# One input load cut by rows, and the output stores cut by batch and by half, in a one-core recurrence and soft-MoE kernel

## Chip, cores and metric

The kernel runs on one core of a Trainium2 chip. The metric is device microseconds (us) of one execution. Beside the times of unprofiled executions there is one profiled execution, from which the views of the trace come; the span is the time from its first to its last instruction.

## The reference

Four sequences of 5056 tokens with 256 channels go through a gated recurrence along the tokens; its output goes through a mixture-of-experts layer with 8 experts of 4 slots each, whose softmaxes run over all 20224 tokens (for the way in) and over the 32 slots (for the way out).

```python
sig = 1.0 / (1.0 + np.exp(-f_logit))
f = lower_bound + (1.0 - lower_bound) * sig
for t in range(S):
    h = f[:, t] * h + (1 - f[:, t]) * x[:, t]
    y[:, t] = h
x = y.reshape(B * S, D)
logits = x @ phi                              # 20224 x 32
d = softmax of logits over the tokens;  c = softmax of logits over the slots
slot_input = d.T @ x                          # 32 x 256
h = relu(slot_input[e] @ w1[e]);  slot_out[e] = h @ w2[e]      # per expert, F = 1024
out = c @ slot_out                            # 20224 x 256
```

All inputs and the output are float32: `x` and `f_logit` 20.7 MB each, the weights 16.8 MB, the output 20.7 MB. No output row can be written before the last weight of the last expert has been used, since every row mixes all slots.

## The kernel before

**First stage, 40 units.** A unit is 512 tokens of one batch. For every pair of units `load` (lines 209 to 226) brings `f_logit` into a tile `f_t` and `x` into a tile `x_t`, on SyncE's DMA queue (SP). Each of the two names has three buffers, so a load waits until the consumer of the tile three pairs earlier is done: ScalarE's sigmoid `gate` (L236, writes `s_t`) for `f_t`, GpSimd's product `enter` (L247, writes `u_t`) for `x_t`. Most pairs are 1024 consecutive tokens of one batch (`long`): one DMA of 128 partitions with 8 KB each, 1 MB (L216). TensorE then turns the tiles to channels on partitions (L251, L266), ScalarE makes the decay `a` (L299, L306), VectorE runs the scan `h` (L334, and L321 for the odd group), TensorE turns `h` back to tokens, and logits, exponentials and slot sums follow. `load(n)` is called six units ahead of its scan. The pair that the change touches, `n = n_unit - 2 * B - 2 = 30`, is the last of the 1 MB pairs; after it come two pairs of 896 KB (L220) and two pairs of two 512 KB DMAs (L226) for each input.

**Weights.** `load_w` (L137, L147) brings the 16 weight tensors (1 MB each in HBM, cast to bfloat16 on the way) on GpSimd's DMA queue. Most of them are issued at the end of the first stage; the last two go into one `f_t` buffer under the name `w_t`, the last of all in two parts of 6/8 and 2/8.

**Experts.** After the slot sums come the two expert products. The last of them, L704, adds up `so_ps` over the experts in order and ends with the two tensors in `w_t`; `slot_out` (L717) is made from it, and `slot_bd` (L719) for two batches side by side.

**Output.** The output of a batch is two blocks of 16 rows per partition (2048 tokens, 2 MB), one block of 7 rows per partition (896 tokens) and 64 tokens left over. TensorE multiplies (L737, L785, L826), VectorE and ScalarE scale into an SBUF tile (`ob` for one batch, `oc` for two), and SP stores it. In order: block 0 of batch 0 in five pieces (`pieces`, L774); the block of 7 rows for batches 0 and 1, then for 2 and 3 (`by_rows`, each stored by `both`, L750, as one DMA of 1792 KB); the 64 left-over tokens (`rest`, L860, two DMAs); block 0 of batches 1, 2, 3 (`whole`, L814, 2 MB each); block 1 of batches 0 and 1 (`couple(1, 0)`, stored by `both`, 4 MB); block 1 of batches 2 and 3 (`couple(1, 1)`, two stores of 2 MB, L843, after all 16 rows are scaled). `couple` walks its 16 rows in eight steps `t` of two rows each.

DMAs of SP are given eight completion semaphores in turn, so each one also waits for the landing of the DMA eight places before it.

Of the kernel before, what the change touches and what calls it, by code (L numbers as in the profile page):

```python
# [18 lines left out]
def kernel(  # L19
# [10 lines left out]
    nc = tc.nc  # L30
    B, S, D = x.shape
# [4 lines left out]
    P = 128  # L36
    DC = D // P
    FC = F // P
    R = 4
    G = P * R  # L40
    n_grp = (S + G - 1) // G
    n_unit = n_grp * B
# [3 lines left out]
    def first(g):  # L46
        return g * G if g < n_grp - 1 else S - G

    def used(g):
        return first(g + 1) - first(g) if g < n_grp - 1 else G  # L50
# [11 lines left out]
    blocks = [(i * P * wide_r, wide_r) for i in range(n_blk)]  # L62
# [105 lines left out]
    with tc.tile_pool(name="sp2", bufs=3) as sp2, \  # L168
# [18 lines left out]
        xs, fs, sts, uts, pss, psus, hs, hps, hts, lgs, ets = ({} for _ in range(11))  # L187
# [4 lines left out]
        def long(n):  # L192
            return B <= n and by_pairs(n)

        def place(n):
            if by_pairs(n):
                t, j = divmod(n, 2 * B)
                return 2 * t + j % 2, j // 2
            return divmod(n, B)
# [4 lines left out]
        def tokens(src, n, k):  # L204
            g, b = place(n)
            v = src[ds(b, k), ds(first(g), G)]
            return v.rearrange("b (p r) d -> p b r d", r=R)

        def load(n, k=2):
            for src, dst, tag in ((f_logit, fs, "f_t"), (x, xs, "x_t")):  # L210
                if n % 2 == 0:
                    dst[n // 2] = ld.tile([P, 2, R, D], F32, name=tag, tag=tag)
                t = dst[n // 2]
                if long(n):
                    g, b = place(n)
                    nc.sync.dma_start(  # L216
                        out=t.rearrange("p u r d -> p (u r) d"),
                        in_=src[b, ds(first(g), 2 * G)].rearrange("(p r) d -> p r d", r=2 * R))
                elif n // B == odd:
                    nc.sync.dma_start(  # L220
                        out=t.rearrange("p u r d -> p (u r d)")[:, ds(0, R7 * D)],
                        in_=src[ds(n % B, 2), ds(first(odd), used(odd))].rearrange(
                            "b (p r) d -> p b (r d)", r=R7))
                else:
                    for m in range(n, n + k):
                        nc.sync.dma_start(out=t[:, ds(m % 2, 1)], in_=tokens(src, m, 1))  # L226
# [256 lines left out]
        for n in range(SINGLE):  # L483
            load(n, 1)
        load(SINGLE)
        lb_constants()
        gate(0, 1)
# [13 lines left out]
        for n in range(n_unit):  # L501
            if n < SINGLE - 2:
# [10 lines left out]
                if n % 2 == 0:  # L513
                    unit(load, n + AHEAD)
# [6 lines left out]
            else:  # L521
# [55 lines left out]
                elif not end and by_pairs(n - 1):  # L577
                    if n % B == 0:
                        g = (n - 1) // (2 * B) * 2
# [50 lines left out]
    with tc.tile_pool(name="ew", bufs=1) as ew, \  # L630
# [34 lines left out]
        for q in range(E // Q):  # L665
# [4 lines left out]
            if q == 0:  # L670
                nc.tensor.matmul(cs_ps, rep2, cs1, start=True, stop=True)
                src = ht_ps.rearrange("p f (j s) -> p f j s", s=NS)[:, :, :, ds(0, SPE)]
                src = bass.AP(tensor=src.tensor, offset=src.offset,
                              ap=[list(src.ap[0]), [P, FC], [NS + SPE, Q], [1, SPE]])
                dst = hid[:, :, :, ds(0, SPE)]
                dst = bass.AP(tensor=dst.tensor, offset=dst.offset,
                              ap=[list(dst.ap[0]), [Q * NS, FC], [NS + SPE, Q], [1, SPE]])
# [3 lines left out]
            for j in range(Q):  # L681
                s0 = (Q + j) * SPE
                src = ht_ps[:, :, ds(j * NS + s0, SPE)]
# [40 lines left out]
    with tc.tile_pool(name="osb", bufs=3) as osb:  # L724
# [18 lines left out]
        def rows_of(i, b):  # L743
            t0, n_r = blocks[i]
            return out[ds(b * S + t0, P * n_r)].rearrange("(p r) d -> p r d", r=n_r)

        def both(i, j, ob):
            t0, n_r = blocks[i]
            dst = out.rearrange("(b t) d -> b t d", b=B)[ds(2 * j, 2), ds(t0, P * n_r)]
            nc.sync.dma_start(out=dst.rearrange("u (p r) d -> p u (r d)", r=n_r),  # L750
                              in_=ob.rearrange("p u r d -> p u (r d)"))

        def first_op():
            n = n_ops[0]
# [22 lines left out]
        def by_rows(i, j):  # L777
            t0, n_r = blocks[i]
            k = ds(j * 2 * NS, 2 * NS)
            ew = etall[k, ds(t0, P * n_r)].rearrange("s (p r) -> s p r", r=n_r)  # L780
            scale = rrow[:, ds(t0 // P, n_r), ds(2 * j, 2)]
            ob = osb.tile([P, 2, n_r, D], F32, name="oc", tag="oc")
            for r in range(n_r):
                op = first_op()
                nc.tensor.matmul(op.rearrange("p u d -> p (u d)"), ew[:, :, r],  # L785
                                 slot_bd[k].rearrange("s u d -> s (u d)"),
                                 start=True, stop=True, skip_group_check=True)
                if r % 2 == 0:
                    by_vector(ob[:, :, r], op, scale[:, r].unsqueeze(2))
                else:  # L790
                    for u in range(2):
                        nc.scalar.activation(ob[:, u, r], op[:, u], ACT.Copy,
                                             scale=scale[:, r, ds(u, 1)])
            both(i, j, ob)
# [21 lines left out]
        def couple(i, j):  # L816
            t0, n_r = blocks[i]
            ew = etall[ds(j * 2 * NS, 2 * NS), ds(t0, P * n_r)].rearrange(
                "s (p r) -> s p r", r=n_r)
            scale = rrow[:, ds(t0 // P, n_r), ds(2 * j, 2)]  # L820
            ob = osb.tile([P, 2, n_r, D], F32, name="oc", tag="oc")
            for t, r in enumerate(range(0, n_r, 2)):
                k = min(2, n_r - r)
                op = pout.tile([P, 2, 2, D], F32, name="op", tag="op")
                for i_r in range(k):
                    nc.tensor.matmul(op[:, i_r].rearrange("p u d -> p (u d)"),  # L826
                                     ew[:, :, r + i_r],
                                     slot_bd[ds(j * 2 * NS, 2 * NS)].rearrange("s u d -> s (u d)"),
                                     start=True, stop=True, skip_group_check=True)
                if t % 2 == 0:  # L830
                    nc.vector.tensor_tensor(  # L831
                        ob[:, :, ds(r, k)].rearrange("p u r d -> p r u d"), op[:, ds(0, k)],
                        scale[:, ds(r, k)].unsqueeze(3).broadcast_to([P, k, 2, D]), ALU.mult)
                else:
                    for i_r in range(k):
                        for u in range(2):
                            nc.scalar.activation(ob[:, u, r + i_r], op[:, i_r, u], ACT.Copy,  # L837
                                                 scale=scale[:, r + i_r, ds(u, 1)])
            if j == 0:
                both(i, j, ob)  # L840
                return
            for u in range(2):
                nc.sync.dma_start(out=rows_of(i, 2 * j + u), in_=ob[:, u])  # L843

        def rest():
            n_p = B // 2
# [18 lines left out]
        for i in range(1, end):  # L865
            for j in range(B // 2):
                couple(i, j)
# [30 lines left out]
```

## Time and profile before

| | before |
|---|---|
| median of 3 runs | 196.5 us (196.48 to 199.11) |
| the profiled execution's own time | 196.45 us |
| its span | 194.7 us |
| mean granted TensorE clock | 0.855 |
| HBM read, written | 58.23 MB, 20.71 MB |
| busy share of the span | PE 77%, VectorE 73%, ScalarE 71%, GpSimd 53% |
| last input load of SP issued | 100.0 us |
| last weight load issued | 124.5 us |
| first output store issued | 143.4 us |
| last output store issued | 176.2 us |

Times inside the execution are microseconds from the start of the span. An engine's busy share is a mean over stages that have different limits, so it doesn't say what bounds a stage. The page's second part cuts the span into 40 equal slices of 4.87 us; its line "DMA" gives the mean busy share of the core's 16 DMA engines in tenths (9 is 90% or more), and "GB/s" what they moved, counted where the data is written, so that a weight load that is cast from float32 to bfloat16 counts with half of what it reads.

### The profile page before, as it was taken

To read this page: it belongs to the slowest core of one execution; us is meant where nothing else is said; L and a number is where in the kernel's file an instruction comes from. 1 tells how busy PE (TensorE), PEld (TensorE's weight loads), DVE (VectorE), ACT (ScalarE), POOL (GpSimd) and SP (SyncE) were. 2 spreads that over 40 slices of the span, in tenths; PEclk is the share of its full clock that TensorE was granted. 3 is DMA by queue.
4 is the path that set the end of the run, shared out by engine and by line. 5 is a ranking of instruction groups with operands and counts; after the bars stand their busy time and mean duration, and the time that the engine had idled before them with its cause. 6 is when DMAs were issued, how large, how long until landed. Compare 5 with 4: busy or idle time off the path is not lost.

```text
span 194.7 us, 3266 instructions
## 1 busy us (share of the span) xinstructions
PE 150.1 (77%) x1216; PEld 106.6 (55%) x1216; DVE 142.2 (73%) x175; ACT 138.9 (71%) x193; POOL 102.5 (53%) x77
## 2 busy tenths in 40 slices
PE   0685897998998979899798976999697999980000
PEld 0464666685776767667585865677461764420000
DVE  2666799899899999999999999543178867770000
ACT  3586888799999999899988698531068688991000
POOL 2586788774999688874979979570030000000000
PEclk9999799699999999999999999999995555555555
DMA  5999999999999999999999999999839999999995
GB/s 206 418 429 429 429 426 419 426 431 373 364 424 424 406 333 428 424 422 358 379 416 414 255 217 213 213 214 216 169 148 428 427 450 431 431 431 431 431 431 222
DMA packets 11953, 70.75 MB, mean 363 GB/s; under 512 B 1297, under 2 KB 1682, under 8 KB 7458
## 3 DMA queue, kind: packets, MB, share of 16 engines
q1 hardware_dynamic: 9456, 62.13, 76.4%
q0 software_dynamic: 2480, 8.42, 21.6%
q8 instruction: 9, 0.15, 0.3%
q14 instruction: 6, 0.05, 0.1%
q10 hardware_dynamic: 2, 0.00, 0.0%
HBM read 58.23 MB, written 20.71 MB: 405 GB/s over the span
## 4 chain that ended last, share of the span: by engine, by line
DMA 31%; PE 26%; DVE 22%; ACT 5%; POOL 3%; issue 3%; SPq 1%; ACTq 0%; POOLq 0%
DVE h L334 11%; DMA f_t<-in_f_logit_dram 10%; DMA w_t<-in_moe_w_dram 10%; PE op L826 7%; DMA x_t<-in_x_dram 6%; PE op L737 6%; DMA w_sb<-in_moe_w_dram 5%; POOL u_t L247 3%; PE sp L251 3%; PE hp L347 3%; DVE h L321 3%; DVE ht L366 3%; PE up L266 3%; DVE oc L727 2%; ACT s_t L236 2%
## 5 line engine op out<-in xcount | busy, mean ns | idle before, releaser
L247 POOL TENSOR_TENSOR u_t<-s_t,x_t 128x1024 bf16<-128x1024 bf16 (+1 forms) x39 | 82.3, 2128 | 22.5 <-ACT s_t L236 13.0
L334 DVE TENSOR_TENSOR_SCAN h<-a,h,up 128x512 bf16<-128x512 f32 x64 | 78.1, 1267 | 6.4 <-PE up L266 2.2
L236 ACT ACTIVATE s_t<-f_t 128x2048 bf16<-128x2048 f32 (+2 forms) x23 | 38.2, 1669 | 4.9 <-DMA f_t<-in_f_logit_dram 4.7
L347 PE MATMUL hp<-ident_f,h 128*128 128x128 f32 (+1 forms) x160 | 29.3, 308 | 8.5 <-DVE ht L366 6.5
L347 PEld LDWEIGHTS hp<-ident_f,h 128*128 128x128 f32 (+1 forms) x160 | 23.6, 207 | 17.7 <-DVE ht L366 11.3
L299 ACT ACTIVATE a<-sp,lbs 128x1024 f32<-128x1024 bf16 x28 | 29.7, 1113 | 2.4 <-PE sp L251 2.4
L251 PE MATMUL sp<-ident_f,s_t 128*128 128x128 f32 x144 | 22.1, 298 | 7.1 <-ACT s_t L236 5.8
L266 PE MATMUL up<-ident_f,u_t 64*128 64x64 f32 x224 | 21.1, 233 | 1.9 <-POOL u_t L247 1.9
L251 PEld LDWEIGHTS sp<-ident_f,s_t 128*128 128x128 f32 x144 | 17.7, 152 | 8.8 <-ACT s_t L236 6.5
L731 ACT ACTIVATE ob<-op,rrow 128x256 f32<-128x256 f32 x32 | 12.4, 478 | 11.7 <-PE op L737 11.3
L266 PEld LDWEIGHTS up<-ident_f,u_t 64*128 64x128 f32 x224 | 16.7, 141 | 6.7 <-issue 2.7
L366 ACT COPY ht<-hp 128x512 f32<-128x512 f32 (+1 forms) x21 | 12.2, 581 | 5.6 <-PE hp L347 5.6
L306 ACT ACTIVATE a<-sp,lbs 128x512 f32<-128x512 bf16 (+2 forms) x16 | 13.2, 868 | 3.1 <-PE sp L251 2.8
L185 PE MATMUL slot_ps<-rep,ident_f 128*128 128x256 f32 x42 | 14.3, 431 | 0.0
L366 DVE COPY ht<-hp 128x512 f32<-128x512 f32 (+1 forms) x19 | 12.7, 670 | 1.2 <-PE hp L347 1.1
L826 PE MATMUL op<-slot_bd,etall 64*128 64x512 bf16 x32 | 13.1, 626 | 0.0
L837 ACT ACTIVATE oc<-op,rrow 128x256 f32<-128x256 f32 x32 | 12.2, 486 | 0.8 <-PE op L826 0.3
L737 PE MATMUL op<-slot_out,etall 32*128 32x256 bf16 x64 | 12.6, 374 | 0.1
L831 DVE TENSOR_TENSOR oc<-op,rrow 128x1024 f32<-128x1024 f32 x8 | 9.7, 1223 | 3.4 <-PE op L826 3.4
L727 DVE TENSOR_TENSOR ob<-op,rrow 128x1024 f32<-128x1024 f32 (+2 forms) x12 | 9.9, 862 | 2.2 <-PE op L737 1.1
L737 PEld LDWEIGHTS <-etall 32*128 32x128 bf16 x64 | 9.0, 152 | 4.0 <-issue 1.7
L380 PE MATMUL lg<-h,phi 128*32 128x512 bf16 (+1 forms) x80 | 10.7, 412 | 0.2 <-ACT et L404 0.2
(109 smaller groups left out, 168.3 us busy)
## 6 DMA issues: line engine op xcount, KB each, us to landing
f_t<-in_f_logit_dram SPq DMA_DIRECT2D x14, 1024.0 KB, 12.3
x_t<-in_x_dram SPq DMA_DIRECT2D x14, 1024.0 KB, 10.6
w_sb<-in_moe_w_dram POOLq DMA_DIRECT2D x14, 512.0 KB, 10.3
out_dram<-ob SPq DMA_DIRECT2D x3, 2048.0 KB, 9.7
f_t<-in_f_logit_dram SPq DMA_DIRECT2D x8, 512.0 KB, 8.6
x_t<-in_x_dram SPq DMA_DIRECT2D x8, 512.0 KB, 7.7
out_dram<-oc SPq DMA_DIRECT2D x1, 4096.0 KB, 14.0
out_dram<-oc SPq DMA_DIRECT2D x2, 2048.0 KB, 15.3
```

The lines of the kernel that those rows point to most:

```text
L185: nc.tensor.matmul(slot_bank[:, 1], ident_f, wide_rep, start=first, stop=False, skip_group_check=True)
L236: nc.scalar.activation(s_t, f_t, ACT.Sigmoid, scale=-1.0)
L247: nc.gpsimd.tensor_tensor(uts[n][:, :r], s_t[:, :r], x_t[:, :r], ALU.mult)
L251: nc.tensor.transpose(ps[:, :, r], t[:, r].bitcast(F32), ident_f)
L266: nc.tensor.transpose(v[:, :, r], t(r)[k].bitcast(F32), ident_f[k, k])
L299: nc.scalar.activation(a, sp[:, :, :, :, o], ACT.Identity, scale=nomlb[:, ds(o, 1)], bias=1.0)
L334: nc.vector.tensor_tensor_scan(h[:, :T, o], decays[n // 2, o][:, n % 2, :T], up[:, :T, o], hs[number(g - 1, b)][:, ds(used(g - 1) - 1, 1), ...
L347: nc.tensor.transpose(hp[:n_p, r], hw[:, :n_p, r], ident_f)
L366: copy(hts[g][:n_p, b].rearrange("p r d -> p (r d)").bitcast(F32), hps.pop(n)[:n_p].rearrange("p r c -> p (r c)"))
L727: nc.vector.tensor_tensor(ob, op, scale.broadcast_to(list(ob.shape)), ALU.mult)
L737: nc.tensor.matmul(op[:, j], ew[:, :, r + j], slot_out[ds(b * NS, NS)], start=True, stop=True, skip_group_check=True)
L826: nc.tensor.matmul(op[:, i_r].rearrange("p u d -> p (u d)"), ew[:, :, r + i_r], slot_bd[ds(j * 2 * NS, 2 * NS)].rearrange("s u d -> s (u d)"),
```

## The change

One load is cut by rows, and five stores are cut in two. The load of `f_logit` for the pair `n = 30` becomes four DMAs into the same tile, of partitions 0 to 111, 112 to 117, 118 to 123 and 124 to 127. `both` issues one DMA for each of its two batches. In `couple(1, 1)` the stores go out after the fourth and after the eighth step, each for eight of the 16 rows of one batch: four DMAs of 1 MB in the place of two of 2 MB. No computation on any engine is changed.

```diff
+        LEAN = (112, 6, 6, 4)
+
         def load(n, k=2):
...
                 if long(n):
                     g, b = place(n)
-                    nc.sync.dma_start(
-                        out=t.rearrange("p u r d -> p (u r) d"),
-                        in_=src[b, ds(first(g), 2 * G)].rearrange("(p r) d -> p r d", r=2 * R))
+                    to = t.rearrange("p u r d -> p (u r) d")
+                    at = src[b, ds(first(g), 2 * G)].rearrange("(p r) d -> p r d", r=2 * R)
+                    p = 0
+                    for k_p in LEAN if n == n_unit - 2 * B - 2 and dst is fs else (P,):
+                        nc.sync.dma_start(out=to[ds(p, k_p)], in_=at[ds(p, k_p)])
+                        p += k_p
...
         def both(i, j, ob):
-            t0, n_r = blocks[i]
-            dst = out.rearrange("(b t) d -> b t d", b=B)[ds(2 * j, 2), ds(t0, P * n_r)]
-            nc.sync.dma_start(out=dst.rearrange("u (p r) d -> p u (r d)", r=n_r),
-                              in_=ob.rearrange("p u r d -> p u (r d)"))
+            for u in range(2):
+                nc.sync.dma_start(out=rows_of(i, 2 * j + u), in_=ob[:, u])
...
+                if j and t % 4 == 3:
+                    h = ds(r - 6, 8)
+                    for u in range(2):
+                        nc.sync.dma_start(out=rows_of(i, 2 * j + u)[:, h], in_=ob[:, u, h])
             if j == 0:
                 both(i, j, ob)
-                return
-            for u in range(2):
-                nc.sync.dma_start(out=rows_of(i, 2 * j + u), in_=ob[:, u])
```

SP issues 71 DMAs in the place of 63: 51 loads (48) and 20 stores (15).

## The prediction

> **What bounds the kernel now.** I read the page's slices first: which resource has no room.
>
> ```profile
> DMA  5999999999999999999999999999839999999995
> GB/s 206 418 429 429 429 426 419 426 431 373 364 424 424 406 333 428 424 422 358 379 416 414 255 217 213 213 214 216 169 148 428 427 450 431 431 431 431 431 431 222
> ```
>
> The 16 DMA engines are busy from the second slice on, except in slices 29 and 30 (136 to 146 us). The dips in GB/s are weight loads, of which only the written half is counted. So there are two DMA-bound stretches, all the loads and all the stores, with a short one between. Which work joins them is in the chain that ended last:
>
> ```profile
> 111.58 10.09 DMA w_sb<-in_moe_w_dram
> 121.96 18.77 DMA w_t<-in_moe_w_dram
> 140.77 1.10 PE so_ps L704 x8
> 141.90 0.49 DVE slot_out L717
> 142.44 0.39 PE op L737 x2
> ```
>
> The last weights land at 140.7 us, 18.8 us after their issue: they wait in the queues, not for an issuer. 2.7 us later (143.41) the first store goes out. The loads' drain, in the DMA view cut to 139 to 142 us (40 slices of 75 ns):
>
> ```profile
> DMA  9989979969879642756666453210000000000800
> ```
>
> The engines run dry one by one over more than a microsecond. The trace's 16 increments of the last transfer's semaphore say the same: 139.71 to 141.44 us, three of them within 0.2 us of the first, four at +0.55 to +0.73, one at +1.07, eight at +1.35 to +1.73, mean +1.0. Of the last store's 16 increments (192.97 to 193.77), 15 lie within 0.28 us. Loads end unevenly, stores nearly level.
>
> Why unevenly: until 5 us the increments of one load lie within 0.25 us of each other. Then one engine falls 0.35 us behind, and after 29.7 us one is 1.3 us behind.
>
> ```profile
> q8 instruction: 9, 0.15, 0.3%
> q14 instruction: 6, 0.05, 0.1%
> q10 hardware_dynamic: 2, 0.00, 0.0%
> ```
>
> Nine instruction blocks of 16 KB go through the same engines, each 0.9 to 1.0 us long, at 29.7, 48.0, 62.5, 79.0, 92.5, 104.9, 124.3, 135.2 and 141.8 us; after each of the first eight one more engine is late, and none catches up, as none is ever idle. The last line is the load of the one-partition `lb_row`: one data packet and one completion packet. One partition used one engine.
>
> **Part 1, the load of 112, 6, 6 and 4 rows.** A 128-row load gives each engine 8 packets of 8 KB; 1 MB landings lie 2.455 us apart, so a row is 2.455/8 = 0.307 us. If 112 rows go 7 to an engine and 6, 6 and 4 rows one to an engine, always on the same first engines, then four engines carry 10 rows (+0.61 us), two carry 9 (+0.31) and ten carry 7 (-0.31). No queue is idle from here to 139 us, so the shift stays until the last weights.
> The small parts' own cost: 512 KB loads land 1.240 us apart and 1 MB loads 2.455, so cutting one in two costs 2 x 1.240 - 2.455 = 0.025 us of engine time; three more on the six engines, 0.075 us.
> The end of the loads is that of the latest engines. Bounds: if all the late ones are among the ten, -0.31 us (the others end at most at +0.73 + 0.61 + 0.08 = +1.42, level with 1.73 - 0.31); if one of the latest is among the four, +0.61 + 0.08 = +0.69 us. The trace doesn't number engines. But each packet starts 3 to 4 ns after the one before it on its engine ended, so up to 47 us its packets can be linked to 16 chains. Eight chains begin at 1.75 to 1.81 us, the others from 2.41 us on. Of the first eight, seven are not late at 47 us, and the eighth got an 8 KB instruction block at 44.7 us; the 16 KB block of 29.7 us and the early 0.35 us fell on chains of the second eight. If engines start in their order, the six that get more are among the early seven. I take -0.31.
>
> [...]
>
> **SP's queue at part 1.** Three more issues of 0.33 to 0.38 us stand ahead of the next `x_t` load and of all that follow:
>
> ```profile
> 73.09 0.33 SPq L216 DMA_DIRECT2D x_t<-in_x_dram  x1
> 73.51 0.38 SPq L216 DMA_DIRECT2D f_t<-in_f_logit_dram  x1
> 77.93 0.33 SPq L216 DMA_DIRECT2D x_t<-in_x_dram  x1
> 78.35 0.66 SPq L220 DMA_DIRECT2D f_t<-in_f_logit_dram  x1
> ```
>
> SP waits from 73.89 to 77.93 for GpSimd's `u_t`: 4.04 us of cover for 1.1. Without it the loads would still lie some 10 us deep in the queues (issue to landing 10 to 12 us). The fourth part must also await the landing eight DMAs back, the `x_t` load of 61.15 + 12.3 = 73.5 us: done by then. With three more DMAs the first odd load comes to wait for the `x_t` load issued at 66.44, landed at about 78.5 against its issue at 78.35; behind it in SP's queue is only the next `x_t`, at 82.84. Its tile is read at 93.1 us. Nothing.
> The reader of the cut load, `s_t`, waits for four landings:
>
> ```profile
> 88.00 1.28 ACT L236 ACT_TABLE_LOAD   x1
> 89.30 1.91 ACT L236 ACTIVATE s_t<-f_t 128x2048 bf16<-128x2048 f32 x1
> ```
>
> The load lands at 85.8 and ScalarE, busy without a gap, starts at 89.3: 3.5 us of slack.
>
> **Part 2, the stores.** The order of rows stays; there are five more DMAs. From 144 us the engines always have work: the last stores are issued at 175.8 us, while the 4 MB store before them (issued 170.1, 14.0 us to landing) lands at 184.1. The half that now goes out some 3 us sooner joins a queue 8 us long: gain 0. Cost: 5 x 0.025 = 0.125 us of engine time, taken from loads since no store shows it alone. SP's extra issues (0.38 us, up to 1.21 in a pair) lie ahead of that backlog; SP waits 4.5 us for `oc` there.
> Smaller packets: the halves have 8 KB per partition for 16 KB.
>
> ```profile
> 16.00:29.00 13.00, 9.95 (x67) 7.49 (x66) 10.93 (x11) 10.67 (x11) 9.33 (x7) 0.87 1.01 429
> 146.00:149.00 3.00, 3.00 (x10) 0.79 (x7) 3.00 (x7) 3.00 (x10) 0.00 (x0) 0.50 1.05 434
> 159.00:173.00 14.00, 14.00 (x41) 6.20 (x40) 10.68 (x9) 12.91 (x35) 0.00 (x0) 0.50 1.00 430
> ```
>
> The last column is GB/s: 8 KB loads 429; the pieces of L774, 4 to 6 KB per partition at a pitch of 16 KB, 434; 16 KB stores 430. The nearest row, the pieces, has the halves' pattern: 0. The other end is 4.19 MB at 429 for 430, +0.02 us. One engine ends each late store 0.5 us after the others; halves could take that away at best: -0.5.
>
> [...]
>
> **Sum.** -0.31 + 0.125 = -0.19 us on the profiled execution, 196.45 (span 194.7, 1.75 around it): 196.26. Its median is 0.05 higher, so I say 196.3.
>
> **Rivals.**
> 1. *The lean falls on late engines, or the 112 rows don't run freely* (0.35). Late engines among the six: +0.31 (one of the two) to +0.69 (one of the four), and +0.125: 196.9 to 197.3. For: eight of 16 are late at the end, and six blocks drawn at random would hardly miss them all. Against: the chains up to 47 us. The same comes out if engines slow each other in the 112 rows, so that seven take as long as eight did: nobody gains, and the six carry +0.31 to +0.69 more. [...]
> 2. *A small part goes through one engine* (0.05). Then 16 rows go to one engine, 23 for 8: 15 x 0.307 = +4.6 us. For: `lb_row` did so with one row. Against: 128-row loads spread evenly. The loads end 4.6 us later if that engine was among the latest, 4.6 - 1.73 = 2.9 if the foremost: 199.5 to 201.2. It is slower by over 2% (200.4) when the engine was already over 0.9 us late, as nine of 16 are.
> 3. *Nothing happens* (0.05): later blocks set which engines end last whatever the load did: 196.45 to 196.6.
>
> The forecast has 0.55, with a range of its own from 195.8 (the 0.5 us of the last engine gained) to 196.6. Over 2%, about what a measurement of this kernel can tell from no change, no case is faster: even perfectly level engines would end the loads only 0.7 us sooner. I leave 0.01 for it, 0.04 for slower (most of rival 2), 0.95 for neither. The range holds the forecast and rivals 1 and 3: 195.8 to 197.4.
>
> **What would show it.** Right: the last `w_t` lands about 0.3 us sooner than 140.7, the busy engines of that drain end closer together, the first store goes out near 143.1, the stores keep 430 GB/s. Wrong: the drain is longer and later (rival 1), by 3 us or more (rival 2); a gap in the DMA slices after 146 us, or `s_t` waiting for `f_t` at 89 us, would break my reading of the covers.

## The result, and the profile after

| | before | after |
|---|---|---|
| median of 6 runs | 196.63 us (196.48 to 199.11) | 201.48 us (200.33 to 202.23) |
| ratio, 95% interval | | 1.0235 (1.0201 to 1.027) |
| the profiled execution's own time, its span | 196.45, 194.7 us | 200.56, 198.8 us |
| weights of the chain that ended last landed | 140.73 us | 144.71 us (+3.98) |
| first output store issued | 143.41 us | 147.33 us (+3.92) |
| last store landed | 193.77 us | 197.86 us (+4.09) |
| first store's issue to last store's landing | 50.36 us | 50.53 us (+0.17) |

The changed kernel is slower by 2.35%. The lower half of the table places the loss: the loads end 4.0 us later, and the stores take 0.17 us more than before. The forecast had -0.31 us for the loads and +0.125 us for the stores.

The page's slices and its packet counts, of the kernel after:

```profile
DMA  6999999999999999999999999999929999999995
GB/s 208 413 433 424 424 435 420 429 424 353 384 430 422 380 362 422 336 238 352 382 419 416 275 241 211 214 214 216 186 79 426 428 441 422 425 422 448 420 422 242
DMA packets 12305, 70.75 MB, mean 356 GB/s; under 512 B 1393, under 2 KB 1778, under 8 KB 7554
```

"DMA" says, as before, that the engines are busy: 9 in all slices but the first, the drain's and the last. "GB/s" says that they moved less while busy: slices 17 to 19 (79.5 to 94.4 us) have 336, 238 and 352, where the slices of before show only one weight load's dip. A packet that takes longer counts as busy all the while (a share of 1.03 at 246 GB/s below), so the busy share alone would have hidden the loss.

The same place in stretches of 2 us, and two stretches of stores; the last column is GB/s, the one before it the DMA share:

```profile
82.00:84.00 2.00, 2.00 (x22) 1.76 (x23) 2.00 (x2) 2.00 (x3) 1.09 (x1) 1.00 1.03 246
84.00:86.00 2.00, 2.00 (x18) 1.18 (x18) 2.00 (x3) 1.98 (x3) 0.63 (x1) 1.00 1.02 238
86.00:88.00 2.00, 1.82 (x15) 1.35 (x14) 2.00 (x3) 1.99 (x3) 2.00 (x2) 1.00 1.03 213
88.00:90.00 2.00, 1.99 (x24) 1.60 (x21) 2.00 (x3) 0.24 (x2) 1.98 (x2) 1.00 0.93 314
149.90:152.90 3.00, 2.72 (x9) 0.77 (x8) 3.00 (x7) 3.00 (x10) 0.00 (x0) 0.73 1.05 433
163.00:177.00 14.00, 14.00 (x42) 6.16 (x41) 10.69 (x9) 12.91 (x35) 0.00 (x0) 0.50 1.00 430
```

The four stretches from 82 to 90 us before:

```profile
82.00:84.00 2.00, 2.00 (x22) 1.73 (x22) 2.00 (x3) 2.00 (x3) 0.91 (x2) 1.00 1.03 434
84.00:86.00 2.00, 2.00 (x19) 1.22 (x16) 2.00 (x2) 1.98 (x3) 2.00 (x1) 1.00 1.00 422
86.00:88.00 2.00, 1.82 (x14) 1.35 (x13) 2.00 (x3) 1.98 (x3) 1.98 (x3) 1.00 1.02 431
88.00:90.00 2.00, 1.89 (x24) 1.50 (x21) 2.00 (x4) 1.99 (x2) 0.76 (x1) 1.00 1.01 400
```

The difference, 188 + 184 + 218 + 86 = 676 GB/s over 2 us each, is 1.35 MB, or 3.2 us at 425 GB/s: most of the 3.98. The stores keep their 430 GB/s. The packets say the same one by one: from 81.5 to 90 us 212 of those of 8 KB take 0.547 us (median) and not 0.309; before, none there takes over 0.35. The cut load has only 128, so whole loads beside it are slowed as well. That is 212 x 0.24 / 16 = 3.2 us, the mean of the 16 engines.

Nothing later gives it back. The chain that ended last:

```profile
125.59 19.12 DMA w_t<-in_moe_w_dram
144.75 1.05 PE so_ps L709 x8
145.82 0.49 DVE slot_out L722
146.36 0.39 PE op L742 x2
```

It is the chain of before, with every step about 4 us later. The loads' drain, in the DMA view cut to 142.7 to 145.7 us:

```profile
DMA  7987979698997666223111111110000000000000
```

The tail at the level of one or two engines is longer: the 16 increments of the `w_t` in that chain lie 2.49 us apart, 1.66 before.

### The profile page after: what moved, and what is told of

It is laid out like the page before. It is cut to its first block, busy times and chain, and to the rows that moved or that the text cites. A ratio compares the mean times of both kernels' runs of the same rounds, so it can differ in the third digit from the quotient of the medians.

```text
span 198.8 us, 3280 instructions
## 1 busy us (share of the span) xinstructions
PE 150.1 (76%) x1216; PEld 106.5 (54%) x1216; DVE 142.1 (72%) x175; ACT 138.6 (70%) x193; POOL 102.5 (52%) x77
## 2 busy tenths in 40 slices
DMA packets 12305, 70.75 MB, mean 356 GB/s; under 512 B 1393, under 2 KB 1778, under 8 KB 7554
## 4 chain that ended last, share of the span: by engine, by line
DMA 32%; PE 22%; DVE 12%; ACT 10%; POOL 7%; issue 5%; SPq 2%; ACTq 0%; POOLq 0%
DMA f_t<-in_f_logit_dram 11%; DMA w_t<-in_moe_w_dram 10%; DVE h L339 7%; PE op L829 7%; POOL u_t L252 6%; DMA x_t<-in_x_dram 6%; DMA w_sb<-in_moe_w_dram 6%; PE op L742 6%; ACT s_t L241 4%; PE sp L256 3%; ACT a L304 3%; PE hp L352 3%; DVE oc L732 2%; DVE ht L371 2%; PE up L271 1%
```

## The experiments

The theories that the expectations name by letters: **A**, engines slow each other on the way into SBUF, by which partitions a load covers (the expectations say that they share ports, the author's assumption: the runs show rates and times of packets, and no port; A1 and A2 are two ways of pricing that, told where they are used). **B**: a row costs what the prediction says, and the loss is in the unequal number of rows on the engines. **C**: reading pieces of 7 rows from HBM is slow. **D**, the number of DMAs: each more costs far more than 0.025 us. The edits are shown against the kernel after, or against the one before with its load cut.

### The two halves of the change alone: `stores_only`, `lean_only`

The first is the kernel after with its loads uncut, the second is the kernel before with only the cut load.

```diff
-                    for k_p in LEAN if n == n_unit - 2 * B - 2 and dst is fs else (P,):
+                    for k_p in (P,):
```

> Only the stores are changed, all loads as before. Every theory that puts the loss into the load (A: engines share write ports of SBUF in a load of 112 rows; B: the extra rows went to engines that were already late; C: reading HBM in pieces of 7 rows is slow; D: more DMAs and issues) expects the time of before plus five more DMAs at 0.025 us: 196.6 us, between 196.4 and 196.9. If the stores carry part of the loss, 198 us or more.

> Only the load of 112, 6, 6 and 4 rows is changed, all stores as before. A, B, C and D all expect the time of the changed kernel less 0.1 us, 200.2 to 202.1 us, with packets of that load and of the next one at 0.5 us in the place of 0.309. If load and stores only cost together, 196.5 us.

Measured: `stores_only` 196.96 us against 196.6 (ratio 1.0015, 1.0001 to 1.003), just above the range expected; from first store to last landing 50.54 us in its trace. `lean_only` 200.26 us (1.0184, 1.0167 to 1.02). The load is 3.66 us of the loss, the stores 0.36. In the trace the stores are only 0.18; the stretch between the last landing and the end of the span varies by 0.4 us from one trace here to the next, so the other 0.18 can't be placed.

### Equal rows, and halves: `r112_16`, `r64_64`

The kernel before, with the one load cut otherwise. `ports` below has 2304 packets under 512 B for 144 DMAs of 128, 112, 64 and 16 rows, 16 for each. Read as one for each engine that took part, and with rows dealt evenly, every engine has 7 + 1 = 8 rows of 112 and 16, and 4 + 4 of 64 and 64.

```diff
-        LEAN = (112, 6, 6, 4)
+        LEAN = (112, 16)
```

> The load as two DMAs of 112 and 16 rows: by the packets of the changed kernel each of the 16 engines then carries 7 + 1 = 8 rows, so that no engine gets more than another. A (shared ports) expects the same loss, +2.8 to +4.5 us, 199.3 to 201.1 us. B (uneven lean) expects no loss, 196.5 us. C (pieces of 7 rows) expects +3 us or more, as A. D (more DMAs) expects 1/3 of the loss at most, 197.8 us.

```diff
-        LEAN = (112, 6, 6, 4)
+        LEAN = (64, 64)
```

> The load as two DMAs of 64 rows, 4 rows to an engine in each, 8 in all. A (shared ports): if pairs of engines write one port, 0.614 us a row for those that meet, a loss of +1.8 to +2.7 us, 198.3 to 199.2 us. [...] B expects no loss, 196.5 us. C (pieces of 7 rows, not a power of two) expects none either, 196.5 us, since an engine reads 4 rows in a run. D expects 197.8 us at most.

Measured: 200.3 us (1.0189, 1.017 to 1.0208) and 201.67 us (1.0267, 1.024 to 1.0293). Equal rows lose as much as the uneven ones: B falls as the cause of the loss here. Halves lose 5.1 us, where C expected nothing: C falls. It is the direction of A, but 1.9 to 2.8 times its price (1.8 to 2.7 us). The stretches from 82 to 86 us in `r64_64` (last column GB/s):

```profile
82.00:84.00 2.00, 2.00 (x22) 1.63 (x23) 2.00 (x3) 2.00 (x3) 1.10 (x1) 1.00 1.03 168
84.00:86.00 2.00, 2.00 (x21) 1.25 (x15) 2.00 (x2) 1.98 (x3) 0.00 (x0) 1.00 1.02 209
```

0.39 and 0.50 of the 434 and 422 of before, at a DMA share of 1.03 and 1.02.

### Four DMAs of all 128 rows: `cols4`

The same load as four DMAs, each of 512 of a partition's 2048 elements.

```diff
+        COLS = (512, 512, 512, 512)
...
-                    for k_p in LEAN if n == n_unit - 2 * B - 2 and dst is fs else (P,):
-                        nc.sync.dma_start(out=to[ds(p, k_p)], in_=at[ds(p, k_p)])
+                    for k_p in COLS if n == n_unit - 2 * B - 2 and dst is fs else (2 * R * D,):
+                        nc.sync.dma_start(out=to.rearrange("p r d -> p (r d)")[:, ds(p, k_p)],
+                                          in_=at.rearrange("p r d -> p (r d)")[:, ds(p, k_p)])
```

> The same load as four DMAs again, but cut along its columns: 128 rows of 2 KB each, so that rows and engines stay as in the load of before. A (shared ports), B and C expect no loss beyond 3 x 0.025 us, 196.5 to 196.8 us. D (more DMAs and issues, completions) expects the loss of the changed kernel, 200 us or more.

Measured: 196.93 us against 196.58 (1.0016, 1.0006 to 1.0026), a little above the range expected. The same stretches as above:

```profile
82.00:84.00 2.00, 1.29 (x11) 1.29 (x12) 2.00 (x4) 1.57 (x2) 1.82 (x1) 1.00 1.04 405
84.00:86.00 2.00, 2.00 (x21) 1.06 (x19) 2.00 (x2) 1.66 (x3) 1.05 (x1) 1.00 1.08 448
```

As many DMAs as in the changed load, a tenth of its loss: D falls. What costs is which partitions a DMA covers.

### Each shape by itself: `ports`

The whole computation is left out. Each stage is 16 loads of one shape into 16 places, then a VectorE copy that waits for them; at the end eight stores of a shape. All have 8 KB per partition, on SP's queue.

```python
def stage(parts):
    for n in range(N):
        for a, k in parts:
            nc.sync.dma_start(out=big[ds(a, k), n], in_=src[n, ds(a, k)])
    settle()
```

> A kernel that leaves the whole computation out and measures loads and stores alone: 16 loads each, 8 KB per row, with a drain after each stage: 128 rows; rows 0 to 63; rows 32 to 95; rows 0 to 111; rows 0 to 111 and then 112 to 127; 128 rows again; then 8 stores each of 128 rows, of rows 0 to 63, of rows 32 to 95, of rows 0 to 111. All theories: 425 to 430 GB/s for 128 rows. A (shared ports): 213 GB/s for rows 0 to 63, 420 for rows 32 to 95, which have as many rows and bytes, and about 250 GB/s for 112 rows with or without the 16. [...] C (pieces of 7 rows from HBM): 425 for rows 0 to 63 and for rows 32 to 95, 250 for 112 rows. A third, fewer rows make each load slower by its fixed cost: the same lower figure for rows 0 to 63 and 32 to 95. For the stores A in its strict form (reading SBUF shares ports as well) expects the same three figures; if only writes into SBUF share, 420 to 430 for all four.

Stretches inside the stages, in the order: loads of rows 0 to 127; 0 to 63; 32 to 95; 0 to 111; 0 to 111 and 112 to 127; 0 to 127 again; stores of rows 0 to 127; 0 to 63; 32 to 95; 0 to 111. The last columns are PEclk, DMA share and GB/s:

```profile
4.00:41.00 37.00, 0.00 (x0) 0.00 (x0) 1.00 1.01 423
46.00:85.00 39.00, 0.00 (x0) 0.00 (x0) 1.00 1.02 207
96.00:109.00 13.00, 0.00 (x0) 0.00 (x0) 1.00 1.01 425
114.00:165.00 51.00, 0.00 (x0) 0.00 (x0) 1.00 1.01 271
172.00:234.00 62.00, 0.00 (x0) 0.00 (x0) 1.00 1.02 251
240.00:277.00 37.00, 0.00 (x0) 0.00 (x0) 1.00 1.00 419
282.00:299.00 17.00, 0.00 (x0) 0.00 (x0) 1.00 1.01 426
302.00:320.00 18.00, 0.00 (x0) 0.00 (x0) 1.00 1.00 208
325.00:334.00 9.00, 0.00 (x0) 0.00 (x0) 1.00 0.99 410
340.00:353.00 13.00, 0.00 (x0) 0.00 (x0) 1.00 1.00 362
```

Rows 0 to 63 run at half the rate and rows 32 to 95 at the full one, with the same bytes and as many packets (16 under 512 B for each DMA), loads and stores alike. The stretch of the 425 leaves out the stage's start, which is slower (307, 258 and 270 GB/s from 88 to 94 us); whole stages of loads take 43.38 and 24.13 us. So it is the place of the rows that decides, as A says. A's 213 and 250 were near what the kernel's stretches had shown (168 to 209 GB/s in `r64_64`, 229 to 250 in `r112_16`, from 82 to 88 us); its 420 for rows 32 to 95 was an assumption that no run had shown before this one. Measured are 207, 425, and 271 and 251. The rows read in HBM move along with the partitions here; that the HBM side is the cause is unlikely, since in `r64_64`, with other HBM addresses, a packet takes as long (0.62 us; 0.64 for rows 0 to 63 here), but no run moved one without the other. The 112 rows have 271 GB/s, and with 16 rows after them 251: 112 rows take longer than 128 (0.92 MB at 271 are 3.39 us, 1.05 MB at 423 are 2.48). On the way out 112 rows lose less, 362 of 426, for which A has no price.

### Cut loads among whole ones: `mix`

The computation is left out. In a stage of 16 loads every second one is cut: by none; 112, 16; 112, 6, 6, 4; 64, 64; 32, 64, 32; none.

```python
def mix(parts):
    for n in range(N):
        for a, k in parts if n % 2 else [(0, 128)]:
            nc.sync.dma_start(out=big[ds(a, k), n], in_=src[n, ds(a, k)])
    settle()
```

> A kernel that leaves the whole computation out: six stages of 16 loads of 1 MB each, with a drain after each stage; in a stage every second load is cut by rows and the others are of 128 rows: no cut; 112 and 16; 112, 6, 6 and 4; 64 and 64; 32, 64 and 32; no cut. Alone, 112 and 16 rows ran at 253 GB/s and 64 rows at 204, which is 4.14 and 5.14 us for 1 MB in the place of 2.47. A1 (only the cut load itself pays): +1.7 us for each 112 and 16, +2.7 for each 64 and 64, so stages 13 and 21 us longer than the uncut 40. A2 (the uncut load beside it pays too, since the engines reach it at different times): +3.5 to +5 us for each, stages 28 to 40 us longer. 32, 64 and 32, of which the middle runs at 420 alone: A1 +1.3, A2 +2.5 or more.

VectorE's timeline; the number in brackets is how long it waited for the stage's loads:

```profile
43.23 0.17 DVE L35 COPY mark<-big 128x16 f32<-128x16 f32 x1 [42.34 <-DMA big<-in_f_logit_dram]
100.99 0.17 DVE L35 COPY mark<-big 128x16 f32<-128x16 f32 x1 [57.59 <-DMA big<-in_f_logit_dram]
176.07 0.17 DVE L35 COPY mark<-big 128x16 f32<-128x16 f32 x1 [74.90 <-DMA big<-in_f_logit_dram]
241.40 0.18 DVE L35 COPY mark<-big 128x16 f32<-128x16 f32 x1 [65.16 <-DMA big<-in_f_logit_dram]
308.93 0.17 DVE L35 COPY mark<-big 128x16 f32<-128x16 f32 x1 [67.35 <-DMA big<-in_f_logit_dram]
```

Divided by eight cut loads: +1.9 us for 112, 16; +4.1 for 112, 6, 6, 4; +2.9 for 64, 64; +3.1 for 32, 64, 32. At the rates of `ports`, 1.05 MB cost 1.05/0.251 - 2.48 = +1.7 for 112, 16 and 1.05/0.207 - 2.48 = +2.6 for 64, 64: near what is measured, so that A1 (only the cut load pays) holds for these two and A2 (the load beside it pays too, 3.5 to 5 us) does not. The last shape costs far more than its parts' own rates would (+1.3, if its 32-row parts run at 207 and the middle at 425), so how neighbouring DMAs overlap counts too. And the price of 112, 16 is only half of the kernel's 3.7. For 112, 6, 6, 4, the change's own cut, it is the other way: 4.1 here and 3.66 in the kernel. So unequal rows, which cost nothing extra in the kernel, do cost here (4.1 against 1.9), where a stage has them eight times; whether they fall on the same engines each time, no run shows.

### Where in the kernel, and how often: `r112_early`, `r112_fx`

The first cuts the load of pair 10 in 112 and 16 rows and not that of pair 30; the second cuts both loads of pair 30, `f_t` and `x_t`.

```diff
-                    for k_p in LEAN if n == n_unit - 2 * B - 2 and dst is fs else (P,):
+                    for k_p in LEAN if n == 2 * B + 2 and dst is fs else (P,):
```

> The cut of 112 and 16 rows moved from the last long load (n = 30) to an early one (n = 10), which lands near 25 us, before the first instruction block delays an engine. A1 (a cut load pays by itself): +1.7 us, 198.3 us. A2 with the engines' lags as the cause of the part beyond it: +1.7 to +2.2 us, since the engines lie within 0.6 us of each other there, against 1.7 us at n = 30. A2 without the lags: +3.7 us, 200.3 us, as at n = 30.

```diff
-                    for k_p in LEAN if n == n_unit - 2 * B - 2 and dst is fs else (P,):
+                    for k_p in LEAN if n == n_unit - 2 * B - 2 else (P,):
```

> Both loads of the pair n = 30, f_logit and x, cut into 112 and 16 rows, one right behind the other. If each cut load costs what the one did: 2 x 3.7 = +7.4 us, 204 us. If part of the loss is at the seams to the uncut loads, which are as many as for one cut load: 1.7 + 3.7 = +5.4 us, 202 us.

Measured: 199.01 us (1.0112, 1.0081 to 1.0143), +2.2; and 204.41 us (1.0374, 1.0329 to 1.0419) against 196.78, +7.6, twice `r112_16`'s 3.7. The idea that the cost sits at the seams between a cut and a whole load, which had 202 us for both loads, falls: each cut load pays in full. And the same cut is 1.5 us cheaper early. One thing that differs between the places is how far the engines have drifted apart: before, the 16 increments of the loads ahead of pair 10 lie 0.6 us apart, and around pair 30 1.7.

### The kernel after once more: `after_again`

> The changed kernel once more, on the chip of the other runs of this group. The sum of its parts as measured alone, 3.66 for the load and 0.36 for the stores, is 200.6 us; its median before was 201.5 (200.3 to 202.2). If the parts add up: 200.4 to 201.2; if load and stores cost something together, 201.5 again.

Measured: 200.68 us (1.0206, 1.017 to 1.0241). The two halves of the change add up to it: 196.6 + 3.66 + 0.36 = 200.6. The first result's median was 0.8 higher, with runs spread over 1.9 us; why is open.

### Level engines: `drain_whole`, `drain_cut`

A small store ahead of the load of pair 30 reads the `x_t` tile that is still to land, so that the queue should run dry and all engines start level (the intent; how level they were is not shown). In `drain_whole` the load is whole, in `drain_cut` cut in 112 and 16 rows.

```diff
+                    if n == n_unit - 2 * B - 2 and dst is fs:
+                        nc.sync.dma_start(out=out[ds(0, 1)],
+                                          in_=xs[n // 2 - 1][ds(0, 1), 0, 0].bitcast(F32))
```

> The kernel of before with one small store of 1 KB ahead of the load at n = 30, which waits until the x_t load before it has landed (its row of the output is written again at the end). All engines are then idle when the load at n = 30 goes out, so that none is late for it; the load is whole. Every theory: some 3 us more than before, 199 to 200.5 us, for the empty queue. It is the base of the next run.

> The same with the load at n = 30 cut into 112 and 16 rows. If the engines' lags at the seam in front of the cut load make its cost 3.7 us in the kernel and 2 us in the stages alone: 1.7 to 2.3 us over the run before it (drain_whole). If something else of the kernel does (the loads behind it, the other tensor, the other engines): 3.2 us or more over it.

Measured: 201.98 us (1.0258, 1.0216 to 1.03) and 202.31 us (1.0329, 1.0256 to 1.0401). Running dry costs 5.4 us by itself, where 3 were expected, so only the two are compared. Their medians are 0.3 us apart, the ratios 1.4, with intervals that overlap, and of the two profiled executions the one with the cut is the faster (202.23 for 203.62 us): the whole times don't price the cut. The traces do at its place: by the median of the 16 increments, the cut load lands 1.37 us later after its issue than the whole one, and the `x_t` load behind it 1.41. The same reading of `r112_16` against the kernel before gives 2.1 and 3.1. So the cut costs about 1.4 us behind the drain, less than either range expected, and 2.1 to 3.1 us without it.

### Late engines by themselves: `lags`

The computation is left out. Each stage is ten loads with the third whole, cut (112, 16) or in halves, twice each; ahead of it no other load, then one of 8 rows, then one of 4, which was meant to make 8 or 4 engines late.

```python
def stage(late, third):
    if late:
        nc.sync.dma_start(out=big[ds(0, late), LAG], in_=src[LAG, ds(0, late)])
    for n in range(10):
        for a, k in third if n == 2 else full:
            nc.sync.dma_start(out=big[ds(a, k), n], in_=src[n, ds(a, k)])
    settle()
```

> A kernel that leaves the whole computation out: 18 stages of ten 1 MB loads, each with a drain after it, of which the third is whole, cut into 112 and 16 rows, or cut into 64 and 64; each kind twice; and this without a small load ahead, then with one of 8 rows, then with one of 4 rows ahead of the ten, which makes 8 or 4 of the 16 engines about 1.2 us late. If the part of the loss that the cut load alone doesn't explain comes from engines that reach the seams at different times, the cut costs 1.5 to 1.9 us (112 and 16) and 2.2 to 2.9 us (64 and 64) in the stages without a late engine, and at least 2.5 us (112 and 16) with late engines. If lateness doesn't matter, the cost is the same in all three, within 0.3 us, and the rest of the loss in the kernel has another cause.

VectorE's timeline, whole and cut, first with no load ahead, then with 8 rows ahead:

```profile
28.36 0.18 DVE L36 COPY mark<-big 128x16 f32<-128x16 f32 x1 [27.47 <-DMA big<-in_f_logit_dram]
56.17 0.17 DVE L36 COPY mark<-big 128x16 f32<-128x16 f32 x1 [27.64 <-DMA big<-in_f_logit_dram]
86.20 0.18 DVE L36 COPY mark<-big 128x16 f32<-128x16 f32 x1 [29.85 <-DMA big<-in_f_logit_dram]
115.81 0.17 DVE L36 COPY mark<-big 128x16 f32<-128x16 f32 x1 [29.43 <-DMA big<-in_f_logit_dram]
...
204.98 0.18 DVE L36 COPY mark<-big 128x16 f32<-128x16 f32 x1 [28.44 <-DMA big<-in_f_logit_dram]
233.07 0.18 DVE L36 COPY mark<-big 128x16 f32<-128x16 f32 x1 [27.92 <-DMA big<-in_f_logit_dram]
262.69 0.18 DVE L36 COPY mark<-big 128x16 f32<-128x16 f32 x1 [29.44 <-DMA big<-in_f_logit_dram]
292.96 0.17 DVE L36 COPY mark<-big 128x16 f32<-128x16 f32 x1 [30.10 <-DMA big<-in_f_logit_dram]
```

The cut costs 29.64 - 27.56 = 2.1 us with no load ahead, 29.77 - 28.18 = 1.6 with 8 rows and 1.8 with 4 rows ahead; the halves 2.5, 2.1 and 2.5. But the small load didn't make engines late by the 1.2 us expected, a figure that no run had shown: in the whole stages the 16 increments of the load just ahead of the third lie 0.3 to 0.5 us apart with it and 0.4 to 0.7 without, and ahead of the cut load in `r112_16` 1.8. So the stages give the price of a cut for engines that are nearly level, 1.6 to 2.1 us, and say nothing of late ones.

## Why the prediction was wrong

**What bounds the kernel: right.** Two DMA-bound stretches joined by the last weights; the 3.98 us that the loads lost came out at the end (+4.09).

**The term that failed:** "If 112 rows go 7 to an engine and 6, 6 and 4 rows one to an engine" and its price of 0.307 us a row. The counts agree with the rows: packets under 512 B grew from 1297 to 1393, by 96, which is five more stores with 16 completion packets each and 6 + 6 + 4 for the small parts, read as one for each engine that took part. That the small parts fall "always on the same first engines", which the -0.31 also needs, no run shows: the trace doesn't number engines. The price did not hold: 212 rows, of this load and of whole loads beside it, took about 0.55 us. The -0.31 was made of a row price taken from 128-row loads, and read as if each engine had a fixed rate of its own; it measured +3.66 (`lean_only`).

**Rival 1 had the cause and not its size.** "The same comes out if engines slow each other in the 112 rows, so that seven take as long as eight did" bounded the slowing at the point where the gain is gone. The 112 rows take longer than 128 by themselves (3.39 us for 2.48, `ports`), and whole loads beside it are slowed too. There was no row for a load of fewer than 128 partitions wider than one, and I set the end of the range at "no gain" where nothing excluded a loss. That engines end unevenly, the other half of rival 1, is not what cost in the kernel: equal rows lose the same. **Rival 2**, a small part on one engine, didn't occur, though its 199.5 to 201.2 us hold the kernel's own profiled time (not its median, 201.48): a right number, by luck, with a mechanism that the packet counts exclude.

**The stores: right in kind, the price low.** +0.17 us in the trace for the forecast's +0.125, and +0.36 by the medians of `stores_only`, at 430 GB/s as said; each of the cut stores spans 128 partitions. A further DMA in a queue with work behind it is cheap here, but 0.025 us is too little: `cols4` has three more for 0.35 us of median (0.19 at the landing of the last weights in its trace).

**The covers didn't hold, and that cost nothing that shows.** I had "3.5 us of slack" for `s_t` and named its waiting as a wrong sign. ScalarE after:

```profile
89.79 1.28 ACT L241 ACT_TABLE_LOAD   x1 [1.76 <-DMA f_t<-in_f_logit_dram]
91.08 1.91 ACT L241 ACTIVATE s_t<-f_t 128x2048 bf16<-128x2048 f32 x1
```

It waits 1.76 us for the late `f_t` and starts at 91.08, not at 89.30. SP, for which the prediction had "Nothing", waits 5.1 us at L225 for landings of `f_t`. But the DMA share stays at 0.93 to 1.07 from 78 to 140 us, until the drain, so the end is set by the loads' own length; the wait is an effect, not the cause.

**What stays open.** That cutting by rows is what costs is shown: `cols4` with as many DMAs loses a tenth, and `ports` shows the slow shapes by themselves. The size is not accounted for. The cut in 112 and 16 rows costs 1.6 to 2.1 us by itself (`ports`, `mix`, `lags`), early in the kernel 2.2, at its place 3.7, and about 1.4 there behind a drain. Engines out of step would fit the traces: with the cut, the whole load ahead of it also lands later after its issue, by 1.8 us in `r112_16` (12.11 for 10.27), 0.4 in `r112_early`, 0.2 to 0.3 in `lags`, the order of the costs; behind the drain there is no load ahead. That lateness is the reason is argued from this order and not shown, since no run changed it alone. No version here beats the kernel before.

## What to carry to other kernels

Where DMA engines are the bound, cut a load along its columns and let each part span all 128 partitions: four such parts cost 0.35 us, four parts by rows 3.7. Before rows are moved from one DMA to another, measure the rate of the new shape by itself: bytes don't price it (0.92 MB in 112 rows took 3.39 us, 1.05 MB in 128 rows 2.48). And a bound of "no gain" needs a reason as much as a gain does.

## What was not expected of the hardware

Sixty-four partitions move at 207 GB/s from row 0 and at 425 from row 32, into SBUF, and at 208 and 410 out of it. A cut load slows whole loads beside it as well (212 slow packets, of which it has 128). And the same cut costs 2.2 or 3.7 us by where it stands in a full queue, and about 1.4 behind a drain.
